# A Fourier transform interleaved with two expert layers: at most two of its steps in a unit, and no cut at a batch's border

## The chip, the core and the metric

The kernel runs as one program on one core of a Trainium2 chip. Its engines are called here TensorE (PE in the rows, PEld for its weight loads), VectorE (DVE), ScalarE (ACT), GpSimd (POOL) and SyncE (SP), which issues most transfers. Each engine works through its own list of instructions in order, and semaphores tie the lists together. The metric is the device time of one execution in microseconds (us).

## The reference, cut to what matters

```
X = fft(fft(x, axis=1), axis=2).real            # x: 8 batches x 3072 tokens x 256
h = X @ w_in                                    # 256 -> 2048, per token
g = max(h, 0) + log1p(exp(-|h|))
y = g @ w_out                                   # 2048 -> 256
e = argmax over 8 experts of cos(y, emb) / tau  # one expert for each token
out = gate(e) * (max(y @ w1[e], 0) @ w2[e])     # 256 -> 1024 -> 256
```

Everything is float32 in and out. Products run in float16 pairs (a high part and a rest), so one logical product is three matmuls.

## The kernel before, in words

The program has two halves. The first half takes the tokens batch by batch through the transform, `w_in`, the softplus, `w_out` and the router, and scatters the rows to buckets of their experts in DRAM. The second half runs the experts over the buckets. The change touches the first half alone.

**Units.** A batch is 8 tiles of 384 tokens, and a tile is worked in 4 units of 512 columns of the hidden layer, so the first half has 256 units, numbered here 0 to 255; unit 32 is the first of batch 1. In each pass of the loop over `s` one unit is started and the work of the two units before it goes on. An order written out by hand (`ORDER`, and `BORD` for the first six units) says in which sequence the pieces are issued, and every engine gets its share of the pieces in that sequence: `sq sp ab f1 pu s1 eu ex pv ev G0 f2 ln p1 G1 r1 g s2 f3 r2 x0 lv ...`. The pieces that matter here:

- `pu`, `pv` are TensorE's products with `w_in`; `eu` is ScalarE's `h<-pu` (L806), once in each unit. `ev` is VectorE's pair L813, L814. `ab`, `ex`, `ln` are ScalarE's three passes (L822, L827, L831), `g` is VectorE's `e<-h,e` (L836), `gh` is GpSimd's high part of it (L847), `lv` VectorE's rest (L860), `G0` to `G2` TensorE's products with `w_out`.
- `f1`, `f2`, `f3` are the three places in a unit at which one step of the transform of the *next* batch may be taken.

**The transform** (`fft_gen`) of one batch has 48 steps. The first 16 belong to `fft_a`: 8 slices k of the input with two steps each (12 small matmuls into `psa`, then ScalarE and VectorE write `U_s`). The other 32 belong to `fft_bc`: 4 steps for each of the 8 tiles (`psb` twice, then `psc`, then `psd`), whose results `pqh`, `pql`, `pq3` are what `pu` and `pv` read in the batch that follows. All steps share one PSUM bank (`psF`).

A slice of the input has to be folded and split before `fft_a` can use it. That goes through three engines in three pieces, without a place among the steps: `sp` folds it (on VectorE, L490 and L492; on GpSimd for some slices, L490, L494, L495), `sa` scales and rounds it on ScalarE (L617, L618, at the unit's end), `sq` makes the rest `xl` on GpSimd (L610, at the start of the next unit). The first of the two steps of a slice marks slice k + 2 for folding.

Before the change, the variable `ph[0]` says in which part the transform is ("a" or "b"), and `fs` lets steps through by it: in part a one step in a unit (in batch 0 two), in part b two, and three in every fourth unit (in batch 0 three). At the first unit of a batch `end_chain` takes whatever steps are left, and a new generator starts. `fft_first` loads the batch after next once more to find its scale.

GpSimd's room in a unit is kept in `room[0]`: with enough of it, GpSimd takes a quarter of VectorE's rest `gl` of that unit as well (`unit_gh`, n = 3).

Of the kernel before, what the change touches and what calls it, by code (L numbers as in the profile page):

```python
# [26 lines left out]
NT = 8  # L27
# [15 lines left out]
P2ON = True  # L43
# [99 lines left out]
def fft_moe_moe(ctx, tc, x, w_in, w128, w_out, emb, tau, w1, w2, fa, db, mcs, tid, ident, tri, misc, out,  # L143
                nbatch=NB):
# [38 lines left out]
    psU = pUV.enter_context(tc.tile_pool(name="psU", bufs=1, space=PSUM, side="right"))  # L183
    psV = pUV.enter_context(tc.tile_pool(name="psV", bufs=1, space=PSUM, side="right"))
    boot = [True, 0, True]
    ph = ["r"]
    late = []
    room = [0.0]
    busy = [False]
# [38 lines left out]
    def job_in_bank(r):  # L228
        ps = fps("pj").rearrange("p (q n) -> p q n", q=4)
        r[0](ps, 0)  # L230
        r[1](ps, 0)

    def run(gen):
        for r in gen:
            if r is not None:
                job_in_bank(r)

    def end_chain(ch):
        if ch.wait:
            for i, (c, r) in enumerate(jobs):  # L240
                if c is ch:
                    job_in_bank(r)
                    del jobs[i]
                    break
            ch.wait = False
        run(ch.gen)
# [324 lines left out]
    def fft_late(b):  # L571
        d = scal[b]
        t = d["t"]
        V.tensor_scalar(t, d["bg"], be_wo, None, op0=ALU.add)
        V.tensor_scalar(t, t, -1.0, 381.0, op0=ALU.mult, op1=ALU.add)
        pow2(d["inv2"], t)
# [25 lines left out]
    def on_v(b, k):  # L602
        return k in (FW1 if b == 1 else FW)
# [27 lines left out]
    def fft_pre(b):  # L631

        x_get(b, 0)
        x_get(b, 1)
        yield
        for k in range(2):
            if boot[0]:
                x_split(b, k)
            else:
                late.append((b, k))  # L640
            yield
        ready.add(b)
# [49 lines left out]
    pq = {}  # L692
# [62 lines left out]

    def fft_gen(b):
        yield from fft_a(b)
        ph[0] = "b"
        for ti in range(NT):
            yield from fft_bc(b, ti)  # L760

    def fft_first(b):
        yield from fft_scale(b)
        yield from fft_pre(b)
# [212 lines left out]
    p2 = {}  # L977
    psH, psO = [], []

    def p2a_open():  # L980
        p2["a"] = a = ctx.enter_context(tc.tile_pool(name="p2a", bufs=2, side="right", reuse_waits="tile"))
        p2["wb"] = [a.tile([128, WE], F16, tag=f"wb{k}", name=f"wb{k}", bufs=1) for k in range(2)]
        p2["tb"] = a.tile([1, 3, NPS + E], F32, tag="tb", name="tb", bufs=1)
        p2["ti"] = a.tile([1, 2, NPS + E], I32, tag="ti", name="ti_", bufs=1)
        p2["cu"] = a.tile([1, 9, E], F32, tag="cu", name="cu", bufs=1)
        p2["cuu"] = a.tile([1, 3, E], U32, tag="cuu", name="cuu", bufs=1)
        p2["snp"] = a.tile([1, 6, E], F32, tag="snp", name="snp", bufs=1)
        p2["sni"] = a.tile([1, 2, 2], I32, tag="sni", name="sni", bufs=1)
        V.memset(p2["snp"][:, 3, :], 0.0)
        p2["zt"] = a.tile([128, RW], F32, tag="zt", name="zt", bufs=1)  # L990
        V.memset(p2["zt"], 0.0)
        V.memset(p2["zt"].bitcast(I32)[:, 264:265], OOB)
# [364 lines left out]
    def chain(*gens):  # L1357
        for g in gens:
            yield from g

    with tc.manual_schedule():
# [85 lines left out]
        sc, scb = Chain(iter(())), [1]  # L1447
        fg = Chain(chain(bg["a"], fft_gen(1)) if nbatch > 1 else bg["a"])
        rq = []
        wp = Chain(iter(()))  # L1450
        for s in range(len(units) + LAG + 1):

            room[0] = ROOM - 2.6 * len(sp3) - 3.4 * sum(not on_v(*t) for t in late)
            nsc = min(len(scq), 2 if cur[0] // 8 >= npair - SNAP or len(scq) > 5 else 1) if room[0] > 0 else 0
            room[0] -= 1.4 * nsc
            busy[0] = bool(sp3) or room[0] < 2.1
            u = units[s] if s < len(units) else None
            if u is not None and u[1] == 0 and u[2] == 0 and 0 < u[0] < nbatch - 1:
                end_chain(fg)
                fg = Chain(fft_gen(u[0] + 1))  # L1460
                ph[0] = "a"
            if s == 4 and nbatch > 1:
                sc = Chain(fft_first(1))
            if u == (nbatch - 1, 0, 0) and P2ON:
                end_chain(fg)
                end_chain(sc)
                pF.close()
                p2a_open()
            cur[0] = s
            if (s == len(units) or ULIM and s == ULIM) and not P2ON:  # L1470
                if s < LAG + 3:
                    ini_ctx.close()
                pUV.close()
                pG.close()
                pF.close()
                p1.close()
                return
            if s == len(units):
                pUV.close()
                p2_psum(0)  # L1480
            if ph[0] == "b" and u is not None and u[0] + 2 < nbatch and scb[0] < u[0] + 2:
                end_chain(sc)
                scb[0] = u[0] + 2
                sc = Chain(fft_first(u[0] + 2))
            boot[2] = s < MB
            if s == LAG + 3:
                run(wo_gen)
                fft_late(0)
                ini_ctx.close()
                wpp = p1.enter_context(tc.tile_pool(name="wpp", bufs=1, reuse_waits="tile"))  # L1490
                rowp.append(wpp)
                wp = Chain(chain(wprep(wpp), snapshot())) if P2ON else Chain(wprep(wpp))
            prev = units[s - 1] if 0 <= s - 1 < len(units) else None
            v = units[s - LAG] if 0 <= s - LAG < len(units) else None

            def x2(tt):
                if v is not None and v[2] == 3:
                    x2_out(v[0], v[1], tt)

            def g2(tt):  # L1500
                if v is not None:
                    while wo_n[0] < 4 * v[2] + 4:
                        boot_w()
                    unit_g2(v, tt)

            def route():
                if rq and not rq[0].step():
                    rq.pop(0)

            def on(fn, lag, *a):  # L1510
                if 0 <= s - lag < len(units):
                    fn(units[s - lag], *a)

            def fs(n):
                first = u is None or u[0] == 0
                if ph[0] == "a" and not (n == 0 or n == 1 and first):
                    return
                if n == 2 and not first and s % 4 != 3:
                    return
                fg.step()  # L1520

            def scs(n):
                if ph[0] != "a" or scb[0] not in ready:
                    if n == 0 or (u is not None and u[0] == 0):
                        sc.step()

            def boot_w():
                if s < LAG + 3:
                    r = next(wo_gen, None)
                    if r is not None:  # L1530
                        job_in_bank(r)

            def cv(k):
                if s < LAG + 3:
                    wi.step(k)

            def uvv():
                if u is not None:
                    uv_v(u)
                elif jobs:  # L1540
                    c, r = jobs.pop(0)
                    job_in_bank(r)
                    c.wait = False

            def tail():
                if "row1" in p2 and (u is None or not S2[0].get("xs")):
                    next(P2, None)

            ops = dict(f1=lambda: fs(0), f2=lambda: fs(1), f3=lambda: fs(2),
                       s1=lambda: scs(0), s2=lambda: scs(1), pu=lambda: on(uv_u, 0), pv=uvv, eu=lambda: on(uv_eu, 0),  # L1550
                       ev=lambda: on(uv_ev, 0), ab=lambda: on(unit_exp, 1), ex=lambda: on(unit_exp2, 1),
                       ln=lambda: on(unit_ln, 1), g=lambda: on(unit_g, 1), gh=lambda: on(unit_gh, 1),
                       lv=lambda: on(unit_gl, 2),
                       G0=lambda: g2(0), G1=lambda: g2(1), G2=lambda: g2(2), x0=lambda: x2(0), x1=lambda: x2(1),
                       x2=lambda: x2(2), r1=route, r2=route, r3=route, sp=split_fold, sa=split_hi, sq=split_lo, wp=wp.step, sc=lambda: scatters(nsc), p1=tail, p2=tail, p3=tail,
                       wo=boot_w, cb=lambda: cv(0), ck=lambda: cv(1), cp=lambda: cv(2))
            for o in BORD[s].split() if s < len(BORD) else ORDER:
                ops[o]()
            if v is not None and v[2] == 3 and (v[0] * NT + v[1]) % 2 == 1:
                rq.append(Chain(router((v[0] * NT + v[1]) // 2)))  # L1560
# [3 lines left out]
        while rq or scq:  # L1564
            if "row1" in p2:
                next(P2, None)
            while jobs:
                c, r = jobs.pop(0)
# [41 lines left out]
```

## Time and profile before

| | |
|---|---|
| median of 3 runs | 3546.36 us (3545.22 to 3548.38) |
| the profiled execution, its own time | 3549.13 us |
| its span, first to last instruction | 3547.4 us |
| granted TensorE clock, mean | 0.957 |
| busy over the span: TensorE, VectorE, ScalarE, GpSimd | 87%, 79%, 64%, 60% |

Times in the rows are us from the span's start unless marked ns. A row of the view by windows has: the stretch, its length, and for each engine its busy us and in brackets its instructions; then the granted clock (1.00 is 2.4 GHz, and an instant is at 2.4 or 1.2 GHz), the share of the DMA engines that is busy, and GB/s. A row of the waits has the waiting instruction, what released it, us in total, times, the longest. A row of the chain has a start, a length and what ran; a row of the groups has the shape, how often, busy us and mean ns, then idle us before it and what ended it. A stretch is cut at the starts of ScalarE's `h<-pu` (L806), of which each unit has one; "unit 9" in the prediction is the time from the start of the one that belongs to unit 9 to the next.

### The profile page before, as it was taken

Reading aid. Unit: us, or ns where it says so; the run is one execution under the profiler, and the core shown is the slowest. Engines: PE = TensorE matmul, PEld = TensorE weight load, DVE = VectorE, ACT = ScalarE, POOL = GpSimd, SP = SyncE. Lnnn points to the kernel's source line nnn. Section 1 sums busy time; section 2 is a strip of 40 time slices with the busy share of each in tenths; the row PEclk is TensorE's granted clock in tenths of the full one; section 3 lists DMA queues with packets and bytes.
Section 4 is the critical chain, followed back from the end, with each engine's and each line's share of the span. In section 5 each row is a group of like instructions: output and inputs, shape, how many; then the busy total and the mean of one; then the engine's idle time right before and its main releaser. Section 6 shows DMA issues by size and latency. Waiting matters only on the chain.

```text
span 3547.4 us, 76364 instructions
## 1 busy us (share of the span) xinstructions
PE 3087.3 (87%) x31264; PEld 2741.2 (77%) x31264; DVE 2820.1 (79%) x4488; ACT 2269.2 (64%) x3400; POOL 2112.4 (60%) x1795
## 2 busy tenths in 40 slices
PE   3776888888888988888898899989789999999997
PEld 3765777777877877777787799977678888888886
DVE  7665899889988998988989988884547777777776
ACT  4665777777867867877888788873334444444443
POOL 5344777667767866777777778763124444444443
PEclk8887999999999999999999999999899999999999
DMA  4110211211211221121120000023653323332231
GB/s 136 46 45 27 71 55 54 70 46 51 86 43 37 65 76 34 45 79 55 46 61 27 27 16 16 20 73 81 175 142 76 74 75 76 79 74 75 74 78 38
DMA packets 197089, 223.74 MB, mean 63 GB/s; under 512 B 119029, under 2 KB 154752, under 8 KB 196481
## 3 DMA queue, kind: packets, MB, share of 16 engines
q1 hardware_dynamic: 177920, 167.32, 17.9%
q0 software_dynamic: 18816, 51.54, 4.2%
q8 instruction: 244, 4.00, 0.5%
q14 instruction: 109, 0.88, 0.1%
HBM read 122.91 MB, written 70.71 MB: 55 GB/s over the span
## 4 chain that ended last, share of the span: by engine, by line
issue 27%; PE 22%; DVE 21%; POOL 14%; ACT 10%; DMA 5%; SPq 0%; POOLq 0%; DVEq 0%; ACTq 0%
PE G L206 9%; DVE e L836 7%; PE pu L206 3%; POOL gh L847 3%; DVE gl L860 3%; POOL out_dram L1235 3%; ACT e L831 3%; PE pv L206 3%; PE psH L206 2%; DVE h L814 2%; ACT e L827 2%; DVE h L813 2%; DMA xt<-in_x_dram 2%; PE psO L206 2%; PE psb L206 1%
## 5 line engine op out<-in xcount | busy, mean ns | idle before, releaser
L847 POOL TENSOR_SCALAR gh<-e,sc 128x1536 f16<-128x1536 f32 (+1 forms) x256 | 617.1, 2411 | 550.6 <-DVE e L836 375.8
L206 PE MATMUL G<-wo_s,gh 128*128 128x264 f16 x6144 | 818.0, 281 | 0.0
L206 PEld LDWEIGHTS <-gh 128*128 128x128 f16 x6144 | 597.6, 100 | 92.2 <-issue 1.3
L206 PE MATMUL psH<-xT,wb 128*128 128x256 f16 (+1 forms) x4992 | 557.2, 273 | 67.7 <-DMA xT<-xs 67.2
L206 PEld LDWEIGHTS <-wb 128*128 128x128 f16 x4992 | 477.7, 100 | 137.6 <-DMA xT<-xs 78.9
L836 DVE SCALAR_TENSOR_TENSOR e<-h,e 128x1536 f32<-128x1536 f32 x256 | 521.8, 2038 | 76.0 <-ACT e L831 72.4
L206 PEld LDWEIGHTS <-win_s 128*128 128x128 f16 x6144 | 541.1, 101 | 43.2 <-issue 19.7
L206 PE MATMUL psO<-wb,hh 128*128 128x256 f16 x3200 | 529.9, 273 | 0.6 <-ACT hh L1209 0.6
L206 PE MATMUL G<-wo_s,gl 128*128 128x264 f16 x3072 | 438.7, 280 | 67.8 <-DVE gl L860 67.5
L860 DVE SCALAR_TENSOR_TENSOR gl<-e,sc,gh 128x1536 f16<-128x1536 f32 (+1 forms) x256 | 470.8, 1839 | 0.0
L1147 POOL TENSOR_TENSOR nr<-ssq,half 128x2 f32<-128x2 f32 (+1 forms) x104 | 238.0, 2289 | 354.9 <-ACT jk L1144 354.6
L206 PE MATMUL psO<-wb,hl 128*128 128x256 f16 x1600 | 436.1, 273 | 0.5 <-DVE hl L1210 0.3
L822 ACT ACTIVATE e<-h 128x1536 f32<-128x1536 f32 x256 | 378.3, 1478 | 70.6 <-DVE h L814 67.2
L1210 DVE SCALAR_TENSOR_TENSOR hl<-psH,hh 128x512 f16<-128x512 f32 (+1 forms) x416 | 268.7, 667 | 178.9 <-ACT hh L1209 172.0
L1209 ACT ACTIVATE hh<-psH 128x512 f16<-128x512 f32 (+1 forms) x416 | 239.7, 579 | 266.1 <-PE psH L206 260.5
L206 PEld LDWEIGHTS <-gl 128*128 128x128 f16 x3072 | 299.7, 99 | 133.2 <-DVE gl L860 84.8
L206 PE MATMUL pu<-pqh,win_s 128*128 128x192 f16 (+1 forms) x2048 | 379.6, 254 | 15.9 <-ACT h L806 15.9
L1235 POOL DMA_INDIRECT out_dram<-ot,r x200 | 202.0, 1010 | 310.0 <-ACT ot L1233 268.9
L831 ACT ACTIVATE e<-e 128x1536 f32<-128x1536 f32 x256 | 379.4, 1482 | 4.6
L827 ACT ACTIVATE e<-e 128x1536 f32<-128x1536 f32 x256 | 378.3, 1478 | 0.0
L206 PEld LDWEIGHTS <-hh 128*128 128x128 f16 x3200 | 312.7, 98 | 36.7 <-ACT hh L1209 0.7
L813 DVE SCALAR_TENSOR_TENSOR h<-pv,sc,h 128x768 f32<-128x768 f32 (+1 forms) x256 | 258.5, 1010 | 99.3 <-PE pv L206 56.8
(274 smaller groups left out, 5912.8 us busy)
## 6 DMA issues: line engine op xcount, KB each, us to landing
xt<-in_x_dram SPq DMA_DIRECT2D x114, 384.0 KB, 3.9
r<-bucket SPq DMA_DIRECT2D x96, 268.0 KB, 3.0
wt<-in_w_dram SPq DMA_DIRECT2D x16, 1024.0 KB
wsc<-wo SPq DMA_DIRECT2D x32, 512.0 KB, 3.0
W<-wsc SPq DMA_DIRECT2D x32, 512.0 KB, 4.5
raw<-in_w_in_dram SPq DMA_DIRECT2D x8, 512.0 KB, 4.4
raw<-in_w_out_dram SPq DMA_DIRECT2D x8, 512.0 KB, 3.7
wb<-wsc SPq DMA_DIRECT2D x2, 2048.0 KB
```

The costliest lines, as they stand in the source:

```text
L206: T.matmul(o, l, r, start=start, stop=stop)
L813: V.scalar_tensor_tensor(h[:, :, n:384], pv[:, :, s0:n], sc["ninv"], h[:, :, s0:n], op0=ALU.mult, op1=ALU.add)
L822: A.activation(e, h, AF.Abs)
L827: A.activation(e, e, AF.Exp, scale=-1.0)
L831: A.activation(e, e, AF.Ln, bias=1.0)
L836: V.scalar_tensor_tensor(flat(d["e"]), flat(d["h"]), 0.0, flat(d["e"]), op0=ALU.max, op1=ALU.add)
L847: G.tensor_scalar(gh[:, 0:n], e[:, 0:n], sg, 1.0, op0=ALU.mult, op1=ALU.mult)
L860: V.scalar_tensor_tensor(flat(d["gl"]), flat(d["e"]), scal[u[0]]["sg"], flat(d["gh"]), op0=ALU.mult, op1=ALU.subtract)
L1147: G.tensor_tensor(nr[:, 0:nt], ssq[:, 0:nt], half[:, 0:nt], op=ALU.pow)
L1209: A.activation(h2, p_, AF.Relu)
L1210: V.scalar_tensor_tensor(l2, p_, 0.0, h2, op0=ALU.max, op1=ALU.subtract)
L1235: no_dep(G.indirect_dma_start(out=out, out_offset=bass.IndirectOffsetOnAxis(ap=rows.bitcast(I32)[:, t, 264:265], axis=0), in_=ot, in_offse ...
```

## The change

Four edits. The transform of the next batch but one is appended to the running generator at a batch's border, in place of `end_chain` and a new one, so that it may run on past the border. `fs` gives no third step from unit 6 on; in part a it gives one step, and a second at `f2` in every eighth unit (below unit 32 in every fourth). The scale pass of a batch goes by the number of the batch that is being transformed (`ph[1]`) and no longer by the unit's batch. The buffers of the second half are opened when the last tile's transform is there, not at a fixed unit.

```diff
-    ph = ["r"]
+    ph = ["r", 0]
...
         yield from fft_a(b)
-        ph[0] = "b"
+        ph[0], ph[1] = "b", b
...
             if u is not None and u[1] == 0 and u[2] == 0 and 0 < u[0] < nbatch - 1:
-                end_chain(fg)
-                fg = Chain(fft_gen(u[0] + 1))
-                ph[0] = "a"
+                fg.gen = chain(fg.gen, fft_gen(u[0] + 1))
...
-            if u == (nbatch - 1, 0, 0) and P2ON:
+            if u is not None and u[0] == nbatch - 1 and P2ON and "a" not in p2 and ((nbatch - 1, NT - 1) in pq or u[1] == NT - 2):
...
-            if ph[0] == "b" and u is not None and u[0] + 2 < nbatch and scb[0] < u[0] + 2:
+            if ph[0] == "b" and ph[1] + 1 < nbatch and scb[0] < ph[1] + 1:
                 end_chain(sc)
-                scb[0] = u[0] + 2
-                sc = Chain(fft_first(u[0] + 2))
+                scb[0] = ph[1] + 1
+                sc = Chain(fft_first(ph[1] + 1))
...
             def fs(n):
-                first = u is None or u[0] == 0
-                if ph[0] == "a" and not (n == 0 or n == 1 and first):
-                    return
-                if n == 2 and not first and s % 4 != 3:
+                if s >= 6 and (n == 2 or n == 1 and ph[0] == "a" and s % 8 != 7 and (s >= 32 or s % 4 != 3)):
                     return
                 fg.step()
```

How the steps lie in the order of the two programs: batch 1 is transformed in units 10 to 28 before and 10 to 38 after (its part a in units 10 to 17 before, 10 to 22 after). Later batches take units 0 to 30 of the batch ahead of them before. After, batches 2, 3, 4 and 5 begin 7, 5, 3 and 1 units late; batches 1 to 4 end in units 6, 4, 2 and 0 of their own batch, batch 5 ends in the unit ahead of its own, and batches 6 and 7 begin and end in the units of before. At the borders the old `end_chain(fg)` finds no step left to take. From unit 224 on the order is the same.

GpSimd, units 10 to 15 (`gh` once in a unit, `xl` for slices 1 to 4 of batch 1). Before:

```order
L847 TENSOR_SCALAR gh_2537<-e_2409,sc_209 128x1536
L610 TENSOR_TENSOR xl_2539<-xt_2246,xh_2533 96x1024
L847 TENSOR_SCALAR gh_2659<-e_2543,sc_209 128x1536
L610 TENSOR_TENSOR xl_2661<-xt_2411,xh_2656 96x1024
L847 TENSOR_SCALAR gh_2784<-e_2665,sc_209 128x1536
L610 TENSOR_TENSOR xl_2786<-xt_2545,xh_2781 96x1024
L847 TENSOR_SCALAR gh_2907<-e_2790,sc_209 128x1536
L610 TENSOR_TENSOR xl_2909<-xt_2667,xh_2904 96x1024
```

And after:

```order
L847 TENSOR_SCALAR gh_2522<-e_2409,sc_209 128x1536
L610 TENSOR_TENSOR xl_2524<-xt_2205,xh_2518 96x1024
L847 TENSOR_SCALAR gh_2644<-e_2528,sc_209 128x1536
L610 TENSOR_TENSOR xl_2646<-xt_2411,xh_2641 96x1024
L847 TENSOR_SCALAR gh_2752<-e_2650,sc_209 128x1536
L610 TENSOR_TENSOR xl_2754<-xt_2589,xh_2749 96x1024
L847 TENSOR_SCALAR gh_2855<-e_2756,sc_209 128x1536
L1338 TENSOR_SCALAR wt_2010<-wt_2010,wps_2511 128x1024
L1339 TENSOR_SCALAR wo_2521<-wt_2010 128x1024
```

Before, every unit has its `xl`; after, about two units in three have one, and the preparation of the expert weights (`wt`, `wo`) stands in a unit between.

TensorE at the head of unit 12, where `pu` of the unit stands behind `f1`'s step. Before:

```order
L206 LDWEIGHTS xh_2656
L206 MATMUL psa_2669<-fa_s_79,xh_2656 128x96
L206 LDWEIGHTS xl_2661
L206 MATMUL psa_2669<-fa_s_79,xl_2661 128x96
L206 LDWEIGHTS win_s_90
L206 MATMUL pu_2684<-pqh_1400,win_s_90 128x192
```

And after:

```order
L206 LDWEIGHTS xh_2518
L206 MATMUL psa_2652<-fa_s_79,xh_2518 128x96
L206 LDWEIGHTS xl_2524
L206 MATMUL psa_2652<-fa_s_79,xl_2524 128x96
L206 LDWEIGHTS win_s_90
L206 MATMUL pu_2667<-pqh_1400,win_s_90 128x192
```

The same place reads slice 2's `xl_2661` before, which GpSimd's list has right behind `gh_2659` of the unit just ended; after, it reads slice 1's `xl_2524`, which stands one `gh` earlier, and `xl_2646` is first read at the head of unit 13.

VectorE in unit 115, one of those with three steps (rows from one `ev` to the next). Before:

```order
L752 SCALAR_TENSOR_TENSOR pq3_14935<-h3_15023,misc_s_64,p3_15021 128x192
L836 SCALAR_TENSOR_TENSOR e_14931<-h_14854,e_14931 128x1536
L713 SCALAR_TENSOR_TENSOR vl_15042<-psb_15043,vh_15041 128x512
L860 SCALAR_TENSOR_TENSOR gl_15058<-e_14814,sc_7969,gh_14927 128x1536
L911 TENSOR_TENSOR rows_14431<-rows_14431,sgn_s_71 128x6x8
L713 SCALAR_TENSOR_TENSOR vl_15042<-psb_15086,vh_15041 128x256
```

And after:

```order
L713 SCALAR_TENSOR_TENSOR vl_14931<-psb_14995,vh_14930 128x256
L836 SCALAR_TENSOR_TENSOR e_14928<-h_14842,e_14928 128x1536
L860 SCALAR_TENSOR_TENSOR gl_14921<-e_14796,sc_8398,gh_14920 128x1152
L911 TENSOR_TENSOR rows_14444<-rows_14444,sgn_s_71 128x6x8
L1313 TENSOR_REDUCE wpm_14918<-wt_14790 128x1
L1316 TENSOR_TENSOR wpm_14918<-wpm_14918 128x1
```

Here VectorE clears the transform's bank three times before and once after, and its `gl` has lost a quarter to GpSimd.

## Rows read from the trace of the kernel before

**Rows 1.** The page's first line.
```profile
span 3547.4 us, 76364 instructions
```

**Rows 2.** Windows: batches 0, 3 and 6 of the first half.
```profile
98.90:487.30 388.40, 290.51 (x2936) 258.10 (x2936) 278.32 (x361) 255.68 (x321) 199.94 (x149) 0.87 0.17 48
...
1065.30:1351.40 286.10, 245.28 (x2651) 217.08 (x2649) 254.36 (x300) 218.95 (x241) 208.98 (x152) 0.97 0.19 57
...
1914.20:2164.60 250.40, 236.83 (x2618) 214.70 (x2617) 224.22 (x234) 205.87 (x220) 196.22 (x170) 0.98 0.07 21
```

**Rows 3.** Windows: units 9 to 16, and 17 to 31, of batch 0.
```profile
210.87:343.45 132.58, 80.78 (x695) 69.99 (x696) 76.20 (x84) 67.07 (x69) 58.13 (x33) 0.77 0.09 27
343.45:487.28 143.83, 121.53 (x1369) 108.57 (x1368) 123.29 (x157) 108.82 (x135) 100.13 (x77) 0.96 0.22 66
```

**Rows 4.** Waits of units 9 to 16.
```profile
POOL gh L847 <- DVE e L836: 47.9, 6, 10.8
...
PE psa L206 <- POOL xl L610: 40.4, 8, 7.4
```

**Rows 5.** The chain of work that ended last, through unit 12 into unit 13.
```profile
265.40 1.76 DVE e L836
...
267.33 3.13 POOL gh L847
270.47 2.52 POOL xl L610
...
273.04 0.98 PE psa L206 x10
274.02 2.56 PE pu L206 x16
...
282.02 1.76 DVE e L836
```

**Rows 6.** ScalarE's timeline: where unit 9 begins and ends.
```profile
210.87 0.90 ACT L806 ACTIVATE h<-pu,sc 128x768 f32<-128x768 f32 x1 [0.18 <-DVE e L836]
...
228.85 0.90 ACT L806 ACTIVATE h<-pu,sc 128x768 f32<-128x768 f32 x1 [2.07 <-PE pu L206]
```

**Rows 7.** Windows: units 0 to 15, then 16 to 31, of batch 3.
```profile
1065.31:1200.59 135.28, 118.45 (x1242) 104.48 (x1240) 124.43 (x127) 106.63 (x104) 98.05 (x66) 0.97 0.15 47
1200.59:1351.38 150.79, 126.80 (x1412) 112.57 (x1411) 129.94 (x174) 112.31 (x137) 110.90 (x86) 0.97 0.22 66
```

**Rows 8.** Groups by shape in batch 3.
```profile
L836 DVE SCALAR_TENSOR_TENSOR e<-h,e 128x1536 f32<-128x1536 f32 x32 | 68.9, 2154 | 7.5 <-ACT e L831 7.2
...
L860 DVE SCALAR_TENSOR_TENSOR gl<-e,sc,gh 128x1536 f16<-128x1536 f32 x25 | 50.4, 2016 | 0.0
...
L860 DVE SCALAR_TENSOR_TENSOR gl<-e,sc,gh 128x1152 f16<-128x1152 f32 x7 | 10.7, 1532 | 0.0
...
L617 ACT ACTIVATE xt<-xt,sc 96x1024 f32<-96x1024 f32 x8 | 9.2, 1145 | 19.1 <-POOL xt L495 18.1 <-DVE xt L492 1.0
...
L492 DVE SCALAR_TENSOR_TENSOR xt<-xt 96x512 f32<-96x512 f32 x5 | 7.6, 1519 | 0.2
...
L490 DVE TENSOR_TENSOR xt<-xt 96x512 f32<-96x512 f32 x5 | 3.7, 743 | 0.0
```

**Rows 9.** Windows: units 16 to 30 of batch 6; units 0 to 19 of batch 7.
```profile
2044.35:2158.65 114.30, 113.03 (x1330) 104.20 (x1328) 98.43 (x113) 94.93 (x112) 94.88 (x93) 1.00 0.05 16
2164.60:2292.43 127.83, 127.83 (x1297) 117.27 (x1295) 113.85 (x112) 108.94 (x95) 97.47 (x90) 1.00 0.06 21
```

**Rows 10.** Windows: a two-step unit of batch 3, and a three-step unit.
```profile
1200.59:1208.13 7.54, 7.54 (x90) 6.80 (x89) 7.36 (x10) 5.90 (x6) 5.65 (x5) 1.00 0.01 2
...
1261.33:1272.09 10.76, 8.10 (x95) 7.04 (x96) 9.66 (x13) 6.51 (x8) 6.05 (x6) 1.00 0.01 2
```

**Rows 11.** VectorE's `e<-h,e`, durations min/median/max: units 9 to 16, then batch 3.
```profile
L836 DVE SCALAR_TENSOR_TENSOR e<-h,e x8: 1736/1758/1759, 216.8 to 330.0; 128x1536 f32<-128x1536 f32 x8
...
L836 DVE SCALAR_TENSOR_TENSOR e<-h,e x32: 1735/1776/4366, 1069.1 to 1345.9; 128x1536 f32<-128x1536 f32 x32
```

## The prediction

> **What bounds the kernel now.** I read first the page's head: a span of 3547.4 us [rows 1], 1.7 us less than the execution's own 3549.13 us, which is 2.8 us over the median of the runs, 3546.36 us. Then I cut the first half into batches by windows. Batch 0 takes 388.40 us, batch 3 286.10, batch 6 250.40 [rows 2]. In batch 6 TensorE is busy 236.83 of 250.40 us: that batch is close to TensorE's own time. In batch 3 VectorE is busy 254.36 of 286.10 us and TensorE 245.28: two engines nearly full, VectorE ahead. In batch 0 no engine is: VectorE, the busiest but TensorE, has 278.32 of 388.40 us. So the question for batch 0 is what makes everybody wait.
>
> Units 9 to 16 answer it. They take 132.58 us, 16.6 us each, with TensorE busy 80.78 us and at a mean granted clock of 0.77 [rows 3]. TensorE waits 40.4 us in 8 waits for GpSimd's `xl`, and GpSimd waits 47.9 us for VectorE's `e` [rows 4]: a ring. The chain of waits walks it: `e` at 265.40, `gh` 3.13 us, `xl` 2.52 us behind it, then TensorE's ten `psa`, then `pu`, then by ScalarE and VectorE the next `e` at 282.02 [rows 5]. One turn is 16.6 us, and each unit makes one, because the step at `f1` needs the `xl` that GpSimd makes behind the `gh` of the unit just ended, and TensorE has `pu` behind that step. In batches 1 to 6 a slice is folded three units ahead of its step, and no such ring turns: units 0 to 15 of batch 3, with the same 16 steps, take 135.28 us, 8.46 each [rows 7].
>
> **The change part by part.** *Part a of batch 1 at a slower pace.* In the order after, slices 2 to 7 are read two units or more behind their fold, so `xl` has a unit to itself and the ring is cut. Slice 0 is still folded in unit 9 and read at the head of unit 10, so unit 9 keeps its 18.0 us (210.87 to 228.85, [rows 6]). Slice 1 moves to `f2` of unit 11, behind `pu`, `pv` and `G0`; I count no wait there. Units 10 to 21, which then hold 15 steps of part a, I price by batch 3's like stretch: 12 x 8.46 = 101.5 us. They fold 7 slices where 12 units of batch 3 fold 4.5; 2.5 more folds at VectorE's 0.743 + 1.519 us [rows 8] are 5.7 us; three more steps 1.7 us (0.58 each, below). That is 109 us.
>
> *Units 22 to 31* then hold 18 steps of part b, near two a unit, as batch 3's second stretch does: 150.79 us over 16 units is 9.42 [rows 7], times 10 is 94.2 us. The same two folds lie in 10 units in place of 16; with a GpSimd fold at 18.1 / 3 = 6.0 us of ScalarE's wait and a VectorE fold at 2.3 [rows 8], 6/16 of 8.3 us is 3 us more, so 97 us. Together units 9 to 31 come to 18 + 109 + 97 = 224 us, against 132.58 + 143.83 = 276.4 now [rows 3]: **52 us less**.
>
> *Fourteen steps carried over* the border (batch 1 has 34 of 48 at unit 31) are done in batches 1 to 4. Their price is bounded below by batch 6, where TensorE sets the time: (114.30 - 15 x 6.39) / 32 = 0.58 us a step, 6.39 being a unit without any transform, 127.83 / 20 [rows 9]; above by batch 3's second stretch, (150.79 - 16 x 6.39) / 32 = 1.52 us, which also carries folds, the scale pass and weight preparation [rows 7, 9]. Those don't come along, so I take 0.75, near the lower end: **10.5 us more** (8 to 21).
>
> *No third step.* A three-step unit of batch 3 takes 10.76 us, a two-step unit 7.54 [rows 10]. The third step itself is only moved (0.75). The other 2.5 us is partly router and weight work that happens to stand there; I credit a fifth, 0.5 us, in three units of each of batches 1 to 5: **8 us less** (0 to 37). Batch 6 gets nothing.
>
> *A quarter of `gl` to GpSimd* in 20 more units: VectorE 2016 - 1532 = 484 ns less each [rows 8], 10 us at most; GpSimd has four instructions for one there, and was busy 98.05 of 135.28 us in such stretches [rows 7]. I take nothing; the bounds are 10 us less and, if GpSimd's extra work (estimated at 2 us a unit from a quarter of `gh` and three small ones) is on the path, 40 more.
>
> *At nothing* also: the dropped `end_chain` (no step was left for it); scale loads, weight loads and scatters, which move by a few units and stay on the same queues (SyncE's loads wait for their buffers, which come free behind `xl` as before); the second half and batch 7, whose order is unchanged. No new wait stands ahead of `pu`: what is late next in batch 0 is VectorE, as in batch 3.
>
> The sum is -52 + 10.5 - 8 = -49.5 us: 3549.1 - 49.5 = 3499.6 for the profiled execution, less 2.8 is 3497 for the median; I say 3498.
>
> **Rivals.** *VectorE and GpSimd block each other more* (slower). In the ring the two take turns: `e` takes 1758 ns at the median and 1759 at most. In batch 3 its median is 1776 but its longest 4366 [rows 11] and its mean 2154 [rows 8]: some wait behind GpSimd. The change lets them run at once in batch 0 and gives GpSimd more quarters of `gl` in batches 1 to 5. `e` and `gl` are 2 x 32 x 6 = 384 instructions in batches 0 to 5; 49.5 us is gone when each is 0.13 us longer. If batch 3's excess of 0.38 us (2154 - 1776) grew by half, 0.19 x 384 = 73 us, the time would be 3498 + 73 = 3571. Against it: little work is added, batch 3's rate in the sum has its own excess in it. Seven in a hundred.
>
> The Trainium skill (SBUF — State Buffer, Who interferes with whom) says that a VectorE instruction with two SBUF inputs and a GpSimd instruction that reads SBUF exclude each other, and the one that came second waits the whole instruction out. By that rule the long `e` are this exclusion; the trace agrees with its form (one shape, 1735 to 4366 ns), and the rule gives no count of meetings, so the sum stays with the rows.
>
> *The ring closes again.* If `xl` is still late in most units of part a (GpSimd has weight preparation and scatters ahead of it now), units 10 to 21 take some 11 us in place of 9, 25 us more: about 3523; at 12.5 us, 41 us more, 3539, which is no change by what can be told here. 0.09 for the first, 0.03 for the second.
>
> *Paid back in full.* The carried steps cost the upper 21 us, the GpSimd folds that now fall together with two scatters (units 104 and 136) and in neighbouring units cost one more 6.0 us stall a batch (24 us), and the three-step units give nothing: -52 + 45 = -7, 3539. 0.03.
>
> *Levelling gives more.* VectorE idles 286.10 - 254.36 = 32 us in batch 3 [rows 2]. If the even spread takes a quarter of that in batches 1 to 5, 40 us in place of the 8 credited: 3466. For it: the three-step units are long; against: the third step was one in 2.25. 0.12.
>
> **How the numbers follow.** Forecast 0.66 (its own range 3475 to 3521), more gain 0.12, ring partly closed 0.09, no change 0.06 (two ways of 0.03), slower 0.07. Below about 0.2% (7 us) a measurement here can't tell a change. Faster is then 0.66 + 0.12 + 0.09 = 0.87, same 0.06, slower 0.07. The range has to leave out no more than 2 in 10: from 3460, which keeps most of the larger gain, to 3535, which keeps the half-closed ring; outside lie the slow rival, no change, and some 0.05 below.
>
> **What would show it.** In the profile after: no wait of `psa` for `xl` but one or two, where 8 stand now; units 9 to 31 near 224 us at a clock near 0.96; batches 1 to 4 a few us to either side of 286; batches 6 and 7 within 2 us; the first half about 50 us shorter and the second the same to 2 us. Wrong would be: the waits gone and the time still there in VectorE's `e` and `gl` (means well over 2154 and 2016 ns), or batches 1 to 4 at 295 or more.

## The result and the profile after

The changed kernel takes 3491.43 us (median of 4 runs, 3485.33 to 3497.28) against 3547.37 us (4 runs, 3545.22 to 3554.46) for the kernel before on the same chip: a ratio of 0.9839, 95% interval 0.9812 to 0.9866. The forecast was 3498 (3460 to 3535). The profiled execution took 3496.98 us. Its page begins, where [rows 1] stood:

```profile
span 3495.2 us, 76414 instructions
```

The windows after, cut like [rows 2, 3]: batch 0; units 9 to 16, 9 to 21 and 22 to 31 of it; batches 2, 3 and 6.

```profile
97.36:432.24 334.88, 270.40 (x2780) 240.65 (x2780) 267.42 (x352) 248.58 (x303) 197.16 (x150) 0.90 0.19 54
208.21:289.06 80.85, 63.61 (x641) 56.05 (x642) 66.26 (x76) 60.38 (x61) 52.17 (x31) 0.92 0.09 26
208.21:332.55 124.34, 101.17 (x1028) 89.53 (x1029) 105.50 (x113) 94.22 (x95) 85.64 (x53) 0.92 0.10 31
332.55:432.24 99.69, 81.39 (x881) 72.15 (x879) 83.97 (x121) 74.80 (x93) 70.48 (x59) 0.93 0.29 86
717.21:1016.28 299.07, 252.65 (x2715) 224.34 (x2713) 252.72 (x309) 222.53 (x250) 222.92 (x168) 0.95 0.18 54
1016.28:1300.09 283.81, 248.09 (x2676) 219.83 (x2676) 251.77 (x314) 219.29 (x247) 215.92 (x167) 0.95 0.19 59
1861.45:2108.33 246.88, 233.70 (x2619) 212.39 (x2617) 220.19 (x234) 205.31 (x219) 190.67 (x170) 0.99 0.07 21
```

Units 9 to 16 fell from 132.58 to 80.85 us, and units 9 to 31 from 276.4 to 124.34 + 99.69 = 224.03. Batch 2, though, became longer by 12 us (286.9 to 299.07), and batch 3 shorter by 2.

The waits of units 9 to 31, which answer to [rows 4]:

```profile
POOL gh L847 <- DVE e L836: 39.0, 12, 6.0
...
PE psa L206 <- POOL xl L610: 11.9, 3, 7.3
```

TensorE waits three times for `xl` (eight times before, in units 9 to 16 alone). GpSimd still waits for `e`, but 3.3 us at a time in place of 8. Unit 9 keeps its length, as ScalarE's `h<-pu` shows (18.4 us; 18.0 in [rows 6]):

```profile
208.21 0.90 ACT L806 ACTIVATE h<-pu,sc 128x768 f32<-128x768 f32 x1
...
226.61 0.90 ACT L806 ACTIVATE h<-pu,sc 128x768 f32<-128x768 f32 x1 [2.07 <-PE pu L206]
```

The groups of batches 1 to 4, which answer to [rows 8]:

```profile
L836 DVE SCALAR_TENSOR_TENSOR e<-h,e 128x1536 f32<-128x1536 f32 x128 | 280.2, 2189 | 37.4 <-ACT e L831 36.6 <-issue 0.2
...
L860 DVE SCALAR_TENSOR_TENSOR gl<-e,sc,gh 128x1536 f16<-128x1536 f32 x86 | 171.2, 1990 | 1.4 <-POOL gap L959 1.4
...
L860 DVE SCALAR_TENSOR_TENSOR gl<-e,sc,gh 128x1152 f16<-128x1152 f32 x42 | 63.3, 1506 | 2.2 <-POOL gh L847 2.2
```

Where the 52.2 us of the span went, from the starts of `h<-pu`: ahead of batch 0 -1.5, batch 0 -53.5, batches 1 to 5 +2.3 (-6.2, +12.2, -2.3, -2.2, +0.8), batch 6 -3.6, batch 7 +1.6, the second half +2.4.

### The profile page after: what moved, and what is told of

It reads as the page before. It is cut to its first block, busy times and chain, and to the rows that moved or that the text cites. A ratio compares the mean times of both kernels' runs of the same rounds, so it can differ in the third digit from the quotient of the medians.

```text
span 3495.2 us, 76414 instructions
## 1 busy us (share of the span) xinstructions
PE 3078.9 (88%) x31264; PEld 2740.8 (78%) x31264; DVE 2796.1 (80%) x4488; ACT 2260.5 (65%) x3400; POOL 2138.7 (61%) x1855
## 4 chain that ended last, share of the span: by engine, by line
issue 29%; PE 24%; DVE 20%; POOL 12%; ACT 10%; DMA 4%; POOLq 0%; SPq 0%; DVEq 0%; ACTq 0%
PE G L206 12%; DVE e L836 5%; PE pu L206 4%; POOL out_dram L1235 3%; DVE gl L860 3%; PE pv L206 3%; ACT e L831 2%; POOL gh L847 2%; ACT e L827 2%; DVE h L814 2%; DVE h L813 2%; PE psb L206 2%; PE psH L206 1%; ACT e L822 1%; POOL xt L495 1%
## 5 line engine op out<-in xcount | busy, mean ns | idle before, releaser
L206 PE MATMUL G<-wo_s,gh 128*128 128x264 f16 x6144 | 832.7, 284 | 2.2 <-POOL gh L850 2.0
L836 DVE SCALAR_TENSOR_TENSOR e<-h,e 128x1536 f32<-128x1536 f32 x256 | 531.6, 2077 | 75.3 <-ACT e L831 71.8
L206 PEld LDWEIGHTS <-win_s 128*128 128x128 f16 x6144 | 534.0, 100 | 24.6 <-DVE h L814 11.6
L860 DVE SCALAR_TENSOR_TENSOR gl<-e,sc,gh 128x1536 f16<-128x1536 f32 (+1 forms) x256 | 451.0, 1762 | 3.6 <-POOL gh L847 2.2
L206 PE MATMUL pu<-pqh,win_s 128*128 128x192 f16 (+1 forms) x2048 | 371.6, 251 | 3.8 <-ACT h L806 3.8
```

The lines of the kernel that those rows point to most:

```text
L206: T.matmul(o, l, r, start=start, stop=stop)
L836: V.scalar_tensor_tensor(flat(d["e"]), flat(d["h"]), 0.0, flat(d["e"]), op0=ALU.max, op1=ALU.add)
L860: V.scalar_tensor_tensor(flat(d["gl"]), flat(d["e"]), scal[u[0]]["sg"], flat(d["gh"]), op0=ALU.mult, op1=ALU.subtract)
```

## The experiments

One table first, since most verdicts rest on it. Ratios are to the kernel before, with 95% intervals, each to runs of it on the same chip (medians from 3546.83 to 3551.59 us), so kernels of different rows are better compared by their ratios than by their medians. The three columns on the right are stretches of the profiled execution, cut at the starts of `h<-pu` (us).

| kernel | median | ratio | units 9 to 31 | batches 1 to 4 | batch 6 |
|---|---|---|---|---|---|
| before | 3547.37 | 1 | 276.4 | 1149.8 | 250.5 |
| changed | 3491.43 | 0.9839 [0.9812, 0.9866] | 224.0 | 1151.3 | 246.9 |
| 1 old pace in batch 0 | 3506.64 | 0.9891 [0.9870, 0.9913] | 270.5 | 1120.8 | 245.9 |
| 2 third step back | 3488.51 | 0.9837 [0.9817, 0.9857] | 223.2 | 1142.6 | 250.1 |
| 3 end at the border | 3486.81 | 0.9837 [0.9815, 0.9860] | 248.4 | 1119.3 | 246.0 |
| 4 `xl` ahead of `gh` | 3525.64 | 0.9931 [0.9906, 0.9956] | 253.4 | 1160.0 | 249.4 |
| 5 changed, once more | 3490.79 | 0.9829 [0.9802, 0.9856] | 221.4 | 1151.7 | 246.9 |
| 6 border, third step | 3497.27 | 0.9853 [0.9829, 0.9877] | 250.3 | 1124.8 | 250.1 |
| 7 border, short end | 3475.70 | 0.9807 [0.9782, 0.9833] | 237.2 | 1119.6 | 247.0 |
| 8 = 7 + later scaling | 3454.23 | 0.9744 [0.9720, 0.9769] | 241.9 | 1114.8 | 245.6 |
| 9 changed + later scaling | 3461.98 | 0.9765 [0.9741, 0.9789] | 224.5 | 1135.1 | 243.3 |
| 10 = 7, no fold on GpSimd | 3466.84 | 0.9764 [0.9743, 0.9785] | 237.7 | 1133.0 | 244.0 |
| 11 before, `wpm` read later | 3563.88 | 1.0041 [1.0027, 1.0055] | 277.4 | 1159.6 | 249.4 |
| 12 = 8, `wpm` read later | 3453.06 | 0.9731 [0.9713, 0.9749] | 239.5 | 1103.8 | 243.2 |

**1. Is it the ring?** Two steps a unit in part a of batch 0, as before; the rest as changed.

```diff
-... and s % 8 != 7 and (s >= 32 or s % 4 != 3)):
+... and s % 8 != 7 and s >= 32):
```

> The changed kernel, with the old pace put back for one thing alone: below unit 32 part a takes two steps in every unit again; third steps stay away and the transform still runs past the border. Theory (the ring of e, gh, xl, psa, pu was the loss): units 9 to 16 turn at 16.6 us again, TensorE waits for xl 8 times, and the whole is about 3491 + 51 - 8 = 3534 us (51 for the ring, 8 back because ten steps fewer are carried into batches 1 to 4). Rival (the gain comes from spreading steps evenly, whatever is folded when): no unit below 32 gets a third step here either, so most of the gain stays: 3500 us or less.

Units 9 to 16 take their old time, and the eight waits are back (the window, then the wait in units 9 to 31):

```profile
208.41:340.90 132.49, 79.64 (x696) 69.22 (x697) 76.63 (x85) 67.11 (x71) 57.95 (x33) 0.78 0.10 27
```

```profile
PE psa L206 <- POOL xl L610: 41.6, 8, 7.4
```

Batch 0 is 46 us longer than in the changed kernel, as the theory of the ring says. The whole is only 15 us longer: batches 1 to 4, which are handed 4 steps in place of 14, are 30 us shorter. Neither theory gives that: handing steps on looks dearer than I had reckoned, which run 3 tries.

**4. The ring cut in another way.** The kernel before, with `sq` (GpSimd's `xl`) issued ahead of `gh` in units 6 to 31.

```diff
-ORDER
+[x for o in ORDER for x in ((["sq"] if o == "gh" and s < 32 else []) + [o])]
```

> The kernel before, with one thing moved: below unit 32 GpSimd makes xl ahead of gh of the same unit, not behind it; pace and border as before. Theory (the ring goes through e and gh): xl no longer waits for e and gh; what is left is a ring by ScalarE's scaling (psa 1.0, pu 2.6, h 0.9, exp and ln 3.0, scaling 2.2, xl 2.1 to 2.5) of about 12 us. Units 9 to 16 fall from 16.6 to 12 or 13 us each, 3547 - 30 = 3517 us (3505 to 3530). Rival (two steps a unit are slow by their own work on VectorE and ScalarE): units 9 to 16 stay above 15.5 us, 3540 us or more.

Units 9 to 16 take 110.46 us with the same steps at the same pace, so 22 us of the stretch were due to the place of `xl` behind `gh`. The waits say what is next in line:

```profile
POOL xl L610 <- ACT xh L618: 38.7, 8, 6.9
...
PE psa L206 <- POOL xl L610: 21.9, 8, 3.1
```

And the chain of work that ended last shows a second, shorter ring without VectorE's `e` in it:

```profile
244.93 0.03 issue
244.95 3.30 POOL xl L610
...
249.28 2.56 PE pu L206 x16
...
255.44 1.48 ACT e L831
256.92 1.04 ACT xt L617
...
257.98 1.06 ACT xh L618
259.05 0.07 issue
259.12 3.04 POOL xl L610
```

From one `xl` to the next it is 14.2 us here and 13.2 in the next turn: ScalarE scales a slice behind its passes over the unit, so a slice that is needed in the next unit still ties the units together. The changed kernel's two slices in three units cut both rings. Batch 1 was 8 us longer here than before (299.2), which I can't explain.

**2. The third step.** The changed kernel with a third step in every fourth unit of part b from unit 32 on.

```diff
-if s >= 6 and (n == 2 or n == 1 and ...
+if s >= 6 and (n == 2 and not (ph[0] == "b" and s >= 32 and s % 4 == 3) or n == 1 and ...
```

> The changed kernel with the third step given back in every fourth unit of part b from unit 32 on; batch 0 is untouched. Theory of the prediction (a three-step unit costs 0.5 us more than its steps): 3491 + 8 = 3499 us, batches 1 to 5 some 8 us longer together. Rival (a step costs the same wherever it stands): 3491 us within 4. Second rival (the excess seen in three-step units was their own, 2.5 us each): 3491 + 30 = 3521 us.

The median is no longer (-3 us, the intervals overlap), and batches 1 to 4 are 8.7 us shorter, batch 6 3.2 us longer. The third step doesn't cost here what I credited. The comparison isn't of the third step alone, though: with it the transform has caught up with the border by batch 3, and batches 3 and 4 (280.4, 280.9 us) are like those of kernel 6 below.

**3. The steps handed on.** The changed kernel with the old cut at the border: steps that are left are done at once in unit 31.

```diff
-fg.gen = chain(fg.gen, fft_gen(u[0] + 1))
+end_chain(fg)
+fg = Chain(fft_gen(u[0] + 1))
```

> The changed kernel with its new pace, but the transform is finished in one go at the border again and the next one started there. Only batch 1 has steps left at its border (14), taken in a row with one PSUM bank between them. Theory: carrying them was needed by the new pace but is no gain by itself; the 14 in a row cost TensorE's 0.6 to 0.9 us and an eviction by ScalarE and VectorE of about 1 us each, some 2 us a step or 28 us with nothing beside it, against 10 us when carried: 3491 + 18 = 3509 us, all of it at units 31 and 32. Rival (carried steps cost batches 1 to 4 more than a lump does): 3491 us or less.

The lump is there: unit 31 takes 36.41 us, at a granted clock of 0.63, where the changed kernel takes 8.5. That lump of 27.9 us is what I had expected of it. But batches 1 to 4 are 32.0 us shorter, which pays for it: the ratio is that of the changed kernel within the intervals, as the rival has it. The windows are batch 2 and the last unit of batch 0:

```profile
738.03:1017.49 279.46, 244.03 (x2651) 216.97 (x2649) 252.37 (x304) 218.28 (x240) 205.82 (x157) 0.98 0.19 59
421.20:457.61 36.41, 22.86 (x226) 18.91 (x226) 14.48 (x20) 12.82 (x25) 9.46 (x9) 0.63 0.04 12
```

Batch 2 is 19.6 us shorter than in the changed kernel; batches 1, 3 and 4 are 4.6, 4.4 and 3.5 us shorter. The changed kernel does 14 steps more in these four batches, four each in batches 1 to 3 and two in batch 4. The 12.4 us over batches 1, 3 and 4 would be 1.2 us a step (an estimate, which puts everything else that moved on the steps), inside the bounds of the prediction. Batch 2 has something else. GpSimd folds 12 slices in these batches in either kernel, but the changed one has only two of them in batch 1 and four in batch 2, where kernel 3 has three. ScalarE's waits for them in batch 2, changed kernel and kernel 3:

```profile
ACT xt L617 <- POOL xt L495: 26.7, 4, 8.4
```

```profile
ACT xt L617 <- POOL xt L495: 14.2, 3, 7.1
```

**5 and 6. Repeat, and the third step without steps handed on.** Run 5 is the changed kernel again: its batches 1 to 6 agree with the first profile within 1.3 us each, so a difference of 3 us in a batch is taken here for a property of the program. Run 6 is kernel 3 with the condition of kernel 2.

> The changed kernel itself, as the measure for the three beside it on the same chip: 3491 us, within 6.

> The kernel that ends the transform at the border (the third experiment), with the third step given back in every fourth unit from unit 32 on. Every batch starts its slices at its unit 0, as in the kernel before, and folds, scale loads, weight work and scatters stand in the same units as without the third step. Theory (a third step costs more than the same step elsewhere): batches 2 to 4 go from 279.5 us back towards the 286 of before, 3487 + 20 to 30 = 3507 to 3517 us. Rival (where folds, scatters and slices meet sets it, not the third step): batches 2 to 4 stay at 279 to 281 us, 3487 us within 4.

Batches 2 to 4 take 279.5, 282.8 and 280.9 us (279.5, 279.4, 280.0 in kernel 3) and batch 6 250.1 (246.0). So the third step (in four units of each batch here) costs 0 to 3.4 us in a batch of the middle, and 4 in batch 6. The median lies between the two theories.

**7 and 8. A shorter lump, and GpSimd's folds.** Kernel 7 is kernel 3 with three steps a unit in part b of batch 0 from unit 23, so that five steps are left at the border in place of 14. Kernel 8 also lets ScalarE scale the slices that GpSimd folds in the middle of the next unit in place of the end of their own; GpSimd makes their `xl` ahead of that unit's `gh`, and its room in the unit counts them.

```diff
-if s >= 6 and (n == 2 or ...
+if s >= 6 and (n == 2 and not (ph[0] == "b" and 22 < s < 32) or ...
```

```diff
...
+held = len(sp2)
 for o in ...:
+    if o == "gh" and held:
+        split_lo()
     ops[o]()
+    if o == "ln" and held:
+        split_hi(held)
```

> The kernel that ends the transform at the border, with three steps a unit in part b below unit 32, so that 5 steps in place of 14 are left for the border. Theory (what batch 0 lost was the ring alone; 14 steps in a row cost 28 us, 5 cost 10, and nine third steps cost their own 0.75 us each): unit 31 falls from 36 to some 18 us, batches 1 to 4 stay at 280 us each, 3487 - 18 + 7 = 3476 us. Rival (third steps in batch 0 cost as much as the lump): 3487 us.

> The seventh experiment's kernel, with one thing moved: for slices that GpSimd folds, ScalarE scales them in the middle of the next unit (behind its ln pass), and GpSimd makes their rest ahead of that unit's gh, where before ScalarE stood waiting for the fold at the end of the same unit. Theory (some 6 us of ScalarE's wait for each of 20 such slices lies on the path): units with a GpSimd fold fall from 12 to 17 us towards 10, 3 to 5 us each, 60 to 100 us in all: 3476 - 60 = 3416 us at best, 3440 at half. Rival (VectorE sets those units, ScalarE's wait is beside it): 3476 us within 6.

Kernel 7 came out as said. Kernel 8 gained 21 us more, 10 of them in batch 5: more than the rival's 6, less than the theory's 36 to 60. In batch 3 unit 5, in which GpSimd folds, falls from 14.74 to 7.53 us; but units 8, 26 and 31 grow from 7.55, 8.73 and 6.11 to 10.20, 10.58 and 12.0, and batches 1 to 4 together give 4.9 us. Much of what one wait gives up another takes; VectorE has 1008 of 1114.75 us of work in these batches.

**9. The same in the changed kernel**, to see whether GpSimd's folds are what batch 2 pays.

> The changed kernel (steps carried, third step gone) with ScalarE's scaling of the slices that GpSimd folds moved to the middle of the next unit. If the carried steps cost through GpSimd's folds standing where ScalarE waits for them, batches 1 to 4 fall from 1151 us to near the 1115 us of the kernel that carries little, and the whole is near 3455. If the carried steps cost by their own work, they stay about 30 us above it and the whole is 3470 or more; with no effect, 3491.

Batches 1 to 4 fall by 16.2 us, about half of the 32, and batch 2 alone by 16.3, to 282.8. (Between kernels 7 and 8 the same edit took 4.9 us from batches 1 to 4, and 2.7 from batch 2.) The whole lies between the two expectations. What it had waited for is seen in ScalarE's timeline of the changed kernel, in two of batch 2's units that took 15.3 and 16.1 us:

```profile
726.01 0.89 ACT L806 ACTIVATE h<-pu,sc 128x772 f32<-128x772 f32 x1
...
737.44 1.15 ACT L617 ACTIVATE xt<-xt,sc 96x1024 f32<-96x1024 f32 x1 [7.45 <-POOL xt L495]
741.33 0.89 ACT L806 ACTIVATE h<-pu,sc 128x772 f32<-128x772 f32 x1
...
800.94 0.88 ACT L806 ACTIVATE h<-pu,sc 128x768 f32<-128x768 f32 x1
...
813.14 1.15 ACT L617 ACTIVATE xt<-xt,sc 96x1024 f32<-96x1024 f32 x1 [8.43 <-POOL xt L495]
817.03 0.88 ACT L806 ACTIVATE h<-pu,sc 128x768 f32<-128x768 f32 x1
```

ScalarE stands 7.45 and 8.43 us at the unit's end before it can scale. In kernel 9 these units and the two other such, 13.5 and 12.8 us, take 8.6, 9.6, 6.9 and 6.5, some 26 us less; 10 of them come back in other units of the batch. The chain of the changed kernel shows why the second is so late: two scatters of rows to the buckets (`bucket`) and the `xl` of the slice before stand ahead of the fold on GpSimd.

```profile
802.57 1.07 POOL bucket L960
...
803.94 0.97 POOL bucket L960
...
804.93 2.14 POOL xl L610
807.06 1.23 POOL xt L490
...
808.38 2.01 POOL xt L494
...
810.47 2.65 POOL xt L495
...
813.14 1.16 ACT xt L617
```

Because batch 3's transform begins 5 units late, its folds stand in other units of batch 2. Batches 3 and 4 of kernel 9 (286.5, 286.7) are 3 us longer than in the changed kernel, which is not explained.

**10. No fold on GpSimd at all** (`FW` and `FW1` name all eight slices).

> The border kernel with three steps late in part b, ScalarE's scaling not moved, and no fold on GpSimd: VectorE does all eight. If VectorE sets these units, 20 folds of about 2.3 us more on it make it 3476 to 3500. If the waits for GpSimd's folds set them (about 6 us each), it is near 3440.

Faster than kernel 7 by 9 us, with intervals that overlap, and between the two theories: batches 1 to 4 are 13.4 us longer, batch 5 17.4 and batch 0 3.9 us shorter. It doesn't decide.

**11 and 12. Weight preparation's maximum.** TensorE's reading of `wpm` (behind L1316) put off by one unit, in the kernel before and in kernel 8.

```diff
 V.tensor_tensor(m[:, 0:1], m[:, 0:1], m[:, 1:2], op=ALU.max)
+yield
+yield
```

> The kernel before, with TensorE's reading of the weight preparation's maximum (wpm) put off by one unit and nothing else. Theory: part of what batches 1 to 4 gain in the kernels that step evenly from the border has nothing to do with the third step; before, TensorE waits 31.0 us in 12 waits for wpm, 4 us of them in the last unit of batches 1 to 4, which takes 10.5 to 12.1 us in place of 6.1. With the wait gone those units fall to about 6 and the whole to 3527 (3515 to 3535). Rival: VectorE is late there anyway and the wait turns up elsewhere, 3547 plus or minus 5.

> The fastest kernel so far (end at the border, three steps in late units of batch 0, later scaling of GpSimd's slices), with the same delay of the reading of wpm. Theory: what the later scaling gained in the units of GpSimd's folds went in part into waits for wpm (44.6 us in 11 waits, and last units of batches 1 to 4 of 12 us where 6 stood); without them 3430. Rival: VectorE, busy over 250 of 277 us a batch, sets these batches, and it stays at 3454 plus or minus 5.

In kernel 11 the wait went and unit 31 of batches 1 to 4 fell to between 5.9 and 6.5 us, as said, yet the kernel is 0.41% slower, which neither theory has. TensorE's waits in batches 1 to 4, first before, then in kernel 11:

```profile
PE pv L206 <- DVE wpm L1316: 27.9, 10, 4.0
...
PE psc L206 <- DVE vl L713: 7.5, 8, 2.8
```

```profile
PE psc L206 <- DVE vl L713: 50.9, 19, 8.8
```

27.9 us went and 43.4 came back at `psc`: the theory fell. But more changed than the wait: GpSimd takes the quarter of `gl` in 54 units of these batches, where it took it in 30, and is busy 874.88 us in place of 829.40, so run 11 isn't a test of the wait alone. In kernel 12 the last units fell from 12 to 6 us and batches 1 to 4 by 11 us, but batch 5 took 5 us of that back, and the median is that of kernel 8 within 1.2 us. Kernels 8 and 12 are the fastest here and beat both kernels.

## Why the prediction was right, and where it wasn't

**The ring, 52 us less: right in size and cause.** Units 9 to 31 were put at 18 + 109 + 97 = 224 us and took 224.03 (units 9 to 21 124.3 for 127, units 22 to 31 99.7 for 97; that two misses of 2.7 us cancel is luck). Putting the pace back brings the ring back (run 1), and moving `xl` alone cuts it (run 4). The clock there was 0.92 to 0.93, not the 0.96 that I named, and three waits for `xl` are left, not two. The rival that the ring closes again is refuted.

**The carried steps, 10.5 us more: mis-sized.** Kernel 3 against the changed kernel puts them at 32.0 us in batches 1 to 4, and run 6 against run 2, with the third step in both, at 1142.6 - 1124.8 = 17.8. It is no fixed price by the step: kernel 1 hands on 4 steps, and its batches 1 to 4 are only 1.4 us longer than kernel 3's. The prediction had priced steps. It had not priced what the handing on shifts: where slices are folded. That was in the rival "paid back in full", as one stall of GpSimd's folds more in each batch. What came is the same 12 folds with longer waits, 69.1 us in place of 58.1 (rows below), and the increase lies in batch 2, which holds four of them. Run 9 supports it: its edit takes 16.3 us from batch 2, where it takes 2.7 without any handing on. Run 2 shows what stays without longer waits: it hands on the same 14 steps, its waits for GpSimd's folds are 57.8 us (59.9 in kernel 6), and its 17.8 us are 1.3 a step (an estimate), inside the bounds. How the 32 us divide exactly is not shown. The condition that I named for being wrong, 295 us or more, was met in batch 2 (299.07) and in no other.

**No third step, 8 us less: the step that failed.** In batches 1 to 4 the third step costs 5.4 us in all where nothing is handed on (run 6 against run 3), and taking it away costs 8.7 where steps are (run 2 against changed). Three-step units are long [rows 10] because of what else stands in them. Where it does show is batch 6, to which I had given nothing: 249.4 to 250.5 us in the five kernels with a third step there, 243.2 to 247.0 in the nine without (some of them with other edits too). With batch 6 counted, run 6 is 7.9 us longer than run 3 over batches 1 to 6, so the size is near the credit where nothing is handed on, but half of it lies where I had put nothing.

**The two errors cancelled, which is luck.** The terms sum to +2.5 us for batches 1 to 5, and these took +2.3. Kernel 3 shows that the true parts are larger and of opposite sign: an even pace that starts at the border makes batches 1 to 4 30.5 us shorter, and handing on takes 32.0 back. What makes the 30.5 is not shown. Not the third step, as run 6 keeps 25 of it; from unit 32 on the steps of that kernel differ from the one before only in the second step of part a in every eighth unit, with which part b starts a unit sooner and has four three-step units in place of three. Two groups of batches 1 to 4 move with the time; here before, in kernel 3 and in the changed kernel (whose `e` stands further up, at 2189 ns):

```profile
L617 ACT ACTIVATE xt<-xt,sc 96x1024 f32<-96x1024 f32 x32 | 36.7, 1146 | 75.5 <-POOL xt L495 71.3 <-DVE xt L492 4.0
...
L836 DVE SCALAR_TENSOR_TENSOR e<-h,e 128x1536 f32<-128x1536 f32 x128 | 275.7, 2154 | 32.3 <-ACT e L831 30.3 <-issue 1.3
```

```profile
L836 DVE SCALAR_TENSOR_TENSOR e<-h,e 128x1536 f32<-128x1536 f32 x128 | 250.2, 1955 | 20.7 <-ACT e L831 19.9
...
L617 ACT ACTIVATE xt<-xt,sc 96x1024 f32<-96x1024 f32 x32 | 36.6, 1143 | 61.4 <-POOL xt L495 58.1 <-DVE xt L492 3.0
```

```profile
L617 ACT ACTIVATE xt<-xt,sc 96x1024 f32<-96x1024 f32 x32 | 36.6, 1142 | 72.0 <-POOL xt L495 69.1 <-DVE xt L492 2.9
```

The last fold of GpSimd in each of these batches stands in unit 28 of kernel 3 and in unit 29 before, and ScalarE waits 4.2 to 5.3 us for it in place of 6.2 to 8.1. `e` takes 25.5 us less in kernel 3 than before. TensorE, too, was busy 12.9 us less for the same matmuls, at a higher clock (before, then kernel 3):

```profile
487.27:1637.06 1149.79, 986.39 (x10599) 871.60 (x10597) 1019.24 (x1212) 875.97 (x960) 829.40 (x608) 0.97 0.19 57
```

```profile
457.61:1576.95 1119.34, 973.51 (x10595) 866.54 (x10594) 1013.67 (x1202) 872.89 (x960) 822.06 (x618) 0.98 0.19 58
```

Which of these is cause and which consequence, no run tells apart. Batch 3 of kernel 3 gains most in its last four units (34.3 us, 44.5 before), where before that fold and a wait for `wpm` stand; run 11, without that wait, gained nothing, but it changed GpSimd's work as well.

**The rival of VectorE and GpSimd blocking each other did not decide between before and after.** `e` takes 2189 ns in the mean over batches 1 to 4 (2154 before, and in [rows 8]), `gl` 1990 (1992 before): 0.035 us on 128 instructions is 4.5 us. The Trainium skill (SBUF — State Buffer, Who interferes with whom) says that such a pair exclude each other; the trace agrees, in that `e` has its old median and single long ones, up to 4910 ns (the view of one line, batches 1 to 4: minimum, median and maximum):

```profile
L836 DVE SCALAR_TENSOR_TENSOR e<-h,e x128: 1736/1759/4910, 436.8 to 1581.5; 128x1536 f32<-128x1536 f32 x128
```

As a part of the 30.5 and the 32.0 us the rival is open: `e` is at 1955 ns in kernel 3, the lowest mean of the kernels here, and so takes 30 us less in all than in the changed kernel (2200 ns in its repeat, run 5). Its length alone doesn't set the time, as VectorE's whole busy time is nearly the same (1019.24 us before, 1013.67 in kernel 3), and kernel 8, shorter than kernel 3, has `e` at 2134.

**At nothing:** batch 7 stayed within 2 us; batch 6 (-3.6) and the second half (+2.4) didn't. The quarter of `gl` was not tried alone.

## What to carry to other kernels

Look for a ring before for a full engine: where no engine is busy and each unit takes the same odd time, walk the chain of waits once around, and give the late piece one more unit; that term can be priced closely from a stretch that already runs at the new pace. In a stretch whose busiest engine has 90% of the time, a wait taken away can come back as another (10 of 26 us in batch 2 of run 9), so a term there needs a run of its own, and two small terms that add up right may each be wrong. When a stream of steps is shifted against the loop, price what is tied to the steps (here folds on a third engine that another engine waits for) at its new place, not only the steps.

## What the runs showed that I had not expected

The second half has the same number of instructions on every engine in every kernel here, and took between 1162.1 and 1172.4 us in the profiled executions (1169.3 and 1172.4 in the two of the changed kernel), while batches 1 to 6 of that kernel agreed within 1.3 us each: a few microseconds can be read by batches that can't be read from the whole. And stretches in which TensorE waits its turn had a low granted clock as well, so that its work took longer there too: 0.63 in the lump of kernel 3, 0.68 in the shorter one of kernel 7 (20.60 us) and 0.77 in the ring [rows 3], against 0.98 in batch 2 of kernel 3.
